# Second pair's k on ScalarE's queue, and the first weight piece rounded one slot later, in a fused attention and MLP kernel

## The chip, the cores and the metric

The kernel runs on one core of a Trainium2 chip. The metric is the device time of one execution in microseconds (us), the median of several runs. A profiled execution also gives its own span, from the first instruction to the last; times inside the kernel are counted from the start of that span.

## The reference

For each of 8 batches and 12 heads, with a sequence of 448 and a head dimension of 64, q and k are divided by their root mean square and scaled by gains, attention is computed with softmax, and the heads are put side by side. The result (3584 x 768) goes through two matrices with a pointwise function between them.

```python
q_n, k_n = (rmsnorm(q, g_q), rmsnorm(k, g_k))
scores = scale * np.matmul(q_n, k_n.transpose(0, 1, 3, 2))
attn = softmax(scores)
x = heads_side_by_side(np.matmul(attn, v))      # 3584 x 768
h = x @ w_in                                     # 768 x 2048, float64
return (h - np.tanh(h)) @ w_out                  # 2048 x 768, float64
```

The softmax and the joining of heads are abbreviated here. q, k and v are float32; the two weight matrices come as float64, and the kernel reads each number as two 32-bit words.

## The kernel before

The work on attention goes pair by pair: a pair is two heads of one batch, so there are 48 pairs, numbered 0 to 47 in this text. The kernel is one program written out by hand for each engine; the order in the source is the order on each engine's queue, and the framework adds the semaphore waits.

Six pairs make a batch. The MLP of a batch can only start when its six pairs are through, so the first batch is computed in "first slots" (`first_slot`, with s from -3 to 5), which have no MLP work beside them. A slot s holds the steps of several pairs: the scores and exps of pair s+1 (`scores`, exps at L504 on ScalarE), the transposes of k and q of pair s+2 (`turn`, L415 and L419 on TensorE, with the copies kT at L417 and qT at L423 on ScalarE), the squares of pair s+3 (`squares`, L123 and L124 on ScalarE, summed at L133 on VectorE, raised to the power -1/2 at L135 on GpSimd), the loads of q and k of pair s+4 and of v of pair s+2, and for pair s the sums over keys (`totals`, L572, with the reciprocal rs at L577), the weighted values (`last_values` L539, `values` L551) and the division (`divide`, L585).

After this, each first slot rounds some of the weights. A weight piece is 256 rows or columns of one half of a matrix: 128 partitions by 768 float64 numbers. There are 32 pieces. `weight_load` fetches the words of a piece; for the first eight pieces they land in the buffer named gT, which has room for four of them. `weight(to)` goes on until `to` pieces have been started: two ScalarE instructions for a piece (`round_weight_a`, L71 and L72), three VectorE instructions for the piece before it (`round_weight_b`, L78, L79, L82), one on GpSimd (`round_weight_c`, L90), and then the loads of up to four pieces ahead. With eight early pieces and six pairs, slot s asks for `weight(s + 3)`: none in slot -3, piece 0 in slot -2, piece 1 in slot -1, and so on. The first load of piece 0 is issued before the slots start.

All loads in question are issued by SyncE (SP). A load of q is one DMA of 224 KB. A load of k is four DMAs: two of 96 KB (L116) and two of 32 KB (L118). A load of v is one of 192 KB (L110) and two of 32 KB (L118). A weight piece of w_in is four DMAs of 192 KB (L265). The framework hands out eight DMA semaphores, in turn; an issue on a semaphore waits until the DMA that used it before has landed.

PSUM has eight banks. Three of them (named mm) are taken in turn by the transposes of k in `turn`, by the totals and by the two value sums; five (named sc) by the scores and by the transposes of q. `turn(s + 2)` in slot s takes the mm bank that the second half of the values of pair s takes again in the same slot, so those values wait for the copy kT.

Of the kernel before, what the change touches and what calls it, by code (L numbers as in the profile page):

```python
# [67 lines left out]
def round_weight_a(nc, raw, dst):  # L68

    lo, hi = raw[:, :, 0], raw[:, :, 1]  # L70
    nc.scalar.activation(dst, hi.bitcast(F32), AF.Abs, scale=2.0**-16)  # L71
    nc.scalar.mul(lo, lo.bitcast(U32), 2.0**-29)  # L72


def round_weight_b(nc, raw, dst):

    bits = dst.bitcast(I32)
    nc.vector.tensor_scalar(out=dst, in0=dst, scalar1=HI_MIN, scalar2=HI_MAX, op0=ALU.max, op1=ALU.min)  # L78
    nc.vector.tensor_scalar(  # L79
        out=bits, in0=bits, scalar1=4, scalar2=1, op0=ALU.logical_shift_left, op1=ALU.logical_shift_right  # L80
    )
    nc.vector.scalar_tensor_tensor(  # L82
        out=bits, in0=raw[:, :, 1], scalar=-(2**31), in1=bits, op0=ALU.bitwise_and, op1=ALU.bitwise_or
    )
# [5 lines left out]
    nc.gpsimd.tensor_tensor(out=bits, in0=bits, in1=raw[:, :, 0], op=ALU.add)  # L90


def fetch(nc, name, t, pair, in_order=False):

    S = pair.shape[1]
    P = 128
    KF, KR = S // P, S % P
    if name == "q":
        nc.sync.dma_start(
            out=t.rearrange("p h c d -> p h (c d)"), in_=pair.rearrange("h (p c) d -> p h (c d)", c=NCH)  # L100
        )
        return
    full, rest = pair[:, : KF * P].rearrange("h (p c) d -> h p c d", c=KF), pair[:, KF * P :]
    if name == "v":
        last = t[:, :, KF]
    if in_order:
        for h in range(2):
            nc.sync.dma_start(out=t[:, h, :KF], in_=pair[h, : KF * P].rearrange("(c p) d -> p c d", p=P))
    elif name == "v":
        nc.sync.dma_start(  # L110
            out=t[:, :, :KF].rearrange("p h c d -> p h (c d)"), in_=full.rearrange("h p c d -> p h (c d)")
        )
    else:
        last = t[:, KF]
        for h in range(2):
            nc.sync.dma_start(out=t[:, :KF, h], in_=full[h])  # L116
    for r in range(2):
        nc.sync.dma_start(out=last[r * KR : (r + 1) * KR], in_=rest.rearrange("h p d -> p h d"))  # L118


def squares_of(nc, sq, n, q, k):
# [16 lines left out]
def bounded_path(tc, ctx, q, k, v, moe_w_in, moe_w_out, out, g_col, ident, ones, half_ones, neg_half, early):  # L138
# [17 lines left out]
    nc = tc.nc  # L156
    B, H, S, D = q.shape
    DFF, DM = moe_w_out.shape
    P = 128
    CP = S // NCH  # L160
    NP = H // 2
    CD, CF = DM // P, DFF // P
    HALF = DM // 2
    FULL = S // P
    REST = S - FULL * P
    steps = [(b, hp) for b in range(B) for hp in range(NP)]
    NS = len(steps)
    EARLY, PIECES = 8, 2 * CF
    HS = S // 2
    HC, HF = CD // 2, CF // 2  # L170
# [4 lines left out]
    KF, KR = S // P, S % P  # L175
# [27 lines left out]
    def mm_bank():  # L203
        return bank_of("mm")
# [3 lines left out]
    def load(s, names):  # L208
        b, hp = steps[s]
        for name in names:  # L210
            src = {"q": q, "k": k, "v": v}[name]
            if s == 0 and name != "v":
                t = early[name]
            else:
                shape = [CP, 2, NCH, D] if name == "q" else [P, NCH, 2, D] if name == "k" else [P, 2, NCH, D]
                t = nat.tile(shape, F32, name=f"{name}_nat", bufs=3 if name == "v" else 2)
                fetch(nc, name, t, src[b, 2 * hp : 2 * hp + 2], by_blocks(s))
            loaded[name, s] = t


# [33 lines left out]
    def weight_load(n):  # L254

        f, i, _ = weight_piece(n)
        if n < EARLY:
            raw = stage[:, n % NSTAGE * 2 * DM : (n % NSTAGE + 1) * 2 * DM]
        else:
            raw = wp.tile([P, 2 * DM], I32, name="w_raw", bufs=3)  # L260
        if n < CF:
            rows = w_in_words[i * HALF : (i + 1) * HALF, f * 2 * P : (f + 2) * 2 * P]
            rows = rows.rearrange("(c h m r) f -> m h r c f", c=HC, h=2, m=2)
            for r in range(4):
                nc.sync.dma_start(  # L265
                    out=raw[r * BL : (r + 1) * BL].rearrange("p (c f) -> p c f", c=HC), in_=rows[r // 2, r % 2]
                )
        else:
            nc.sync.dma_start(
                out=raw.rearrange("p (f c) -> p f c", f=2),  # L270
                in_=w_out_words[f * P : (f + 2) * P, 2 * i * HALF : 2 * (i + 1) * HALF].rearrange(
                    "(f p) c -> p f c", p=P
                ),
            )
        raws[n] = raw.rearrange("p (n w) -> p n w", w=2)

    def weight_dst(n):
        return weight_piece(n)[2].rearrange("p f n -> p (f n)")
# [5 lines left out]
    def place_free(n):  # L284

        if n < EARLY:
            return n - NSTAGE < done[2]
        return n - 3 < max(done[2], EARLY)

    def weight(to):  # L290

        while done[1] < min(to, PIECES):
            n = done[1]
            round_weight_a(nc, raws[n], weight_dst(n))
            if n:
                round_weight_b(nc, raws[n - 1], weight_dst(n - 1))
            done[1] = n + 1
            finish_weights(n)
            while done[0] < min(n + 4, PIECES) and place_free(done[0]):
                weight_load(done[0])  # L300
                done[0] += 1
            if kept[1] < kept[0] and n >= 4 * kept[0] + 2:
                keep_weights()
        if done[1] == PIECES > done[2]:
            round_weight_b(nc, raws[PIECES - 1], weight_dst(PIECES - 1))
            finish_weights(PIECES)

    def finish_weights(to):
        while done[2] < to:
            round_weight_c(nc, raws.pop(done[2]), weight_dst(done[2]))  # L310
            done[2] += 1
            if done[2] % 4 == 0 and done[2] <= CF:
                combine_weights(done[2] // 4 - 1)
            keep_w_out(done[2] - 2)
# [14 lines left out]
    def keep_weights():  # L329
        j = kept[1]  # L330
        for p in ORDER:
            nc.sync.dma_start(out=w_in_dram[j, p].rearrange("p (f n) -> p f n", f=2), in_=built(j, p))
        kept[1] = j + 1
# [59 lines left out]
    def squares(s):  # L393
        squares_of(nc, early["sq"], early["n"], loaded["q", s], loaded["k", s])
# [35 lines left out]
    def by_blocks(s):  # L430
        return has(s) and steps[s][0] >= FIRST
# [51 lines left out]
    def sc_bank():  # L483
        return bank_of("sc")

    def scores(s, c):

        rr, kT, qT = turned[s]
        halves, keys, n = (1, P, S) if c < KF else (2, KR, HS)
        name, bufs = ("p", 2) if c < 2 else ("p_full", 1) if c < KF else ("p_last", 2)  # L490
        if c == 1:
            p = probs[s, 1] = probs[s, 0]
        else:
            p = probs[s, c] = pp.tile([P, 2, 2 if c < 2 else 1, n], F32, name=name, bufs=bufs)
        tiles = [sc_bank() for _ in range(2)]
        for i in range(halves):
            for h in range(2):
                r = slice(h * D, (h + 1) * D)
                nc.tensor.matmul(  # L499
                    tiles[h][i * keys : (i + 1) * keys, :n], lhsT=kT[r, c * P : c * P + keys],  # L500
                    rhs=qT[r, i * n : (i + 1) * n], start=True, stop=True,
                )
        for h in range(2):
            nc.scalar.activation(  # L504
                p[:, h, c if c < 2 else 0, :], tiles[h][:, :n], AF.Exp,
                scale=1.0 if rr is None else rr[:, 0, 2 * c + h : 2 * c + h + 1],
            )
# [339 lines left out]
    def has(s):  # L847
        return 0 <= s < NS

    def first_slot(s):  # L850

        if has(s + 1):
            scores(s + 1, 0)
            scores(s + 1, 1)
        if has(s + 2):
            turn(s + 2, mm_bank(), sc_bank())
        if s > -3:
            load(s + 4, "qk")
        if s > -3:
            squares(s + 3)  # L860
        norm(s + 3)
        if has(s):
            totals(s, mm_bank())
        if has(s + 2):
            load(s + 2, "v")
        if has(s + 1):
            scores(s + 1, KF)
        if has(s):
            av = [mm_bank() for _ in range(2)]
            last_values(s, av)  # L870
            values(s, av)
        if has(s + 1):
            scores(s + 1, 2)
            add(s + 1)
            add_last(s + 1)
        norm_q(s + 3)
        if s == -3:
            early["g_col"]()
        if has(s):
            divide(s, av)  # L880
        weight(EARLY * (s + 3) // (NP + 2))
        combine(2)

    def early_slot(s):
# [432 lines left out]
```

## Time and profile before

| what | value |
|---|---|
| time, 3 runs | 1428.47, 1431.7, 1432.04 us; median 1431.7 us |
| span of the profiled execution | 1429.6 us |
| TensorE matmul busy, 0 to 1429.6 us | 1396.1 us |
| TensorE idle, 0 to 20 us | 11.2 us of 20 |
| ScalarE idle, 0 to 30 us | 12.9 us of 30 |
| DMA traffic, whole span | 249.73 MB, 175 GB/s |

The idle times come from the busy times of ten-microsecond windows: TensorE was busy 2.07 and 6.71 us in the first two, and ScalarE 3.91, 5.53 and 7.71 us in the first three. A busy time is a sum over instructions; it says nothing on which of them the end of the program hangs. For that there is the chain of waits, which goes back from the last instruction to what released it, step by step. In the middle and at the end of the span that chain runs along TensorE; at the start it goes through other engines and transfers.

### The profile page before, as it was taken

The page shows a single profiled execution, that of the slowest core. Times are in us where ns is not written, and L with a number is a line of the kernel's source. Part 1 is how long each engine was busy: PE and PEld are TensorE (multiplying, and loading weights), DVE is VectorE, ACT ScalarE, POOL GpSimd, SP SyncE. Part 2 cuts the span into 40 slices and gives each one's busy share as a digit, 9 for nine tenths or more (in the row PEclk, how much of TensorE's full clock was granted, in tenths as well). Part 3 has the DMA queues.
Part 4 walks back from the last instruction along what each step waited for, and adds up shares of the span by engine and source line. Part 5 has one row for each costly group of instructions (what it writes and reads, how often), then busy time and mean ns, then how long its engine had stood idle before and what let it go on. Part 6 is the DMA issues. An engine that isn't in the chain of part 4 may idle for free.

```text
span 1429.6 us, 25681 instructions
## 1 busy us (share of the span) xinstructions
PE 1396.1 (98%) x10032; PEld 1174.7 (82%) x10032; DVE 867.8 (61%) x1396; ACT 412.0 (29%) x790; POOL 530.6 (37%) x348
## 2 busy tenths in 40 slices
PE   6999899999999999999999999999999999999997
PEld 3568654478998899889889988988998898899997
DVE  3999889856645676556755567546765577522311
ACT  5765454233311322222221223113221222201100
POOL 4656555232521345215533246313452145401310
PEclk9999899999999999999999999999999999999999
DMA  8769787864666656765657666666566656365663
GB/s 184 171 187 248 245 236 203 223 195 127 171 178 152 169 158 170 174 171 164 173 150 189 161 153 178 180 152 164 162 172 173 169 161 183 115 181 171 189 194 89
DMA packets 355254, 249.73 MB, mean 175 GB/s; under 512 B 266484, under 2 KB 297396, under 8 KB 355124
## 3 DMA queue, kind: packets, MB, share of 16 engines
q1 hardware_dynamic: 355120, 248.00, 64.0%
q8 instruction: 81, 1.33, 0.4%
q14 instruction: 49, 0.40, 0.1%
q10 hardware_dynamic: 4, 0.00, 0.0%
HBM read 214.50 MB, written 33.42 MB: 173 GB/s over the span
## 4 chain that ended last, share of the span: by engine, by line
PE 91%; DVE 3%; DMA 2%; SPq 1%; ACT 1%; issue 0%; POOL 0%; ACTq 0%
PE mm L640 66%; PE sc L499 9%; PE sc L551 6%; PE mm L805 4%; PE sc L572 2%; PE sc L539 2%; DMA k_nat<-in_k_dram 1%; DMA w_raw<-in_moe_w_out_dram 1%; DVE w_out L82 1%; DVE w_out L324 1%; DVE rs L577 1%; PE mm L551 1%; DMA gT<-in_moe_w_in_dram 0%; PE sc L419 0%; SPq L265 0%
## 5 line engine op out<-in xcount | busy, mean ns | idle before, releaser
L640 PE MATMUL mm<-xT,w_f 128*128 128x224 f32 x1392 | 275.6, 354 | 0.0
L640 PEld LDWEIGHTS mm<-xT,w_f 128*128 128x128 f32 x1392 | 262.1, 190 | 9.1 <-issue 7.8
L640 PE MATMUL mm<-gT,w_f 128*128 128x224 f32 x1344 | 263.0, 354 | 0.0
L640 PEld LDWEIGHTS mm<-gT,w_f 128*128 128x128 f32 x1344 | 252.8, 190 | 11.4 <-issue 9.1
L457 POOL TENSOR_TENSOR rr_mine<-rr_mine,neg_half 128x28 f32<-128x28 f32 x30 | 145.0, 4835 | 256.1 <-DVE rr_mine L456 256.1
L640 PE MATMUL mm<-tt,w_f 128*128 128x224 f32 x1044 | 208.7, 353 | 0.0
L640 PEld LDWEIGHTS mm<-tt,w_f 128*128 128x128 f32 x1044 | 197.0, 190 | 3.9 <-issue 3.9
L640 PE MATMUL mm<-tg,w_f 128*128 128x224 f32 x1008 | 197.7, 352 | 0.0
L677 POOL TENSOR_TENSOR gT<-s,th 128x448 f32<-128x448 f32 x96 | 122.6, 1284 | 200.6 <-ACT th L676 198.5
L640 PEld LDWEIGHTS mm<-tg,w_f 128*128 128x128 f32 x1008 | 190.6, 190 | 0.0
L499 PE MATMUL sc<-qT,kT 64*128 64x448 f32 (+1 forms) x960 | 168.1, 499 | 12.0 <-ACT p_last L504 8.1
L499 PEld LDWEIGHTS sc<-qT,kT 64*128 64x128 f32 (+1 forms) x960 | 71.2, 167 | 83.6 <-issue 50.0
L600 POOL TENSOR_TENSOR tt<-xT,tt 128x224 f32<-128x224 f32 x23 | 17.1, 744 | 232.2 <-DVE xT L585 232.1
L676 ACT ACTIVATE th<-s 128x448 f32<-128x448 f32 x96 | 55.6, 579 | 135.3 <-DVE s L706 55.6
L577 DVE RECIPROCAL rs<-sc 128x224 f32<-128x224 f32 x42 | 65.3, 1556 | 42.6 <-PE sc L572 42.5
L504 ACT ACTIVATE p<-sc 128x448 f32<-128x448 f32 x120 | 55.6, 550 | 109.1 <-PE sc L499 109.1
L135 POOL TENSOR_TENSOR rr<-rr,neg_half 112x8 f32<-112x8 f32 (+1 forms) x36 | 59.6, 1676 | 56.8 <-DVE rr L134 56.5
L551 PE MATMUL sc<-p,v_nat 128*32 128x224 f32 x1344 | 79.1, 353 | 0.0
L805 PE MATMUL mm<-gT,w_out 128*128 128x448 f32 x192 | 76.8, 557 | 0.0
L585 DVE TENSOR_TENSOR xT<-sc,rs 64x224 f32<-64x224 f32 x168 | 65.2, 388 | 9.7 <-PE sc L551 2.3
L464 DVE TENSOR_TENSOR qk_n<-qk_nat,rr_mine 128x896 f32<-128x896 f32 x30 | 46.4, 1546 | 39.3 <-POOL rr_mine L457 38.7
L805 PEld LDWEIGHTS mm<-gT,w_out 128*128 128x128 f32 x192 | 37.0, 196 | 37.6 <-issue 36.2
(136 smaller groups left out, 1630.9 us busy)
## 6 DMA issues: line engine op xcount, KB each, us to landing
w_f<-w_in SPq DMA_DIRECT2D x196, 384.0 KB, 3.2
w_f<-w_out SPq DMA_DIRECT2D x147, 512.0 KB, 4.0
w_raw<-in_moe_w_out_dram SPq DMA_DIRECT2D x16, 768.0 KB, 5.1
out_dram<-th SPq DMA_DIRECT2D x192, 56.0 KB, 1.9
w_in<-w_out SPq DMA_DIRECT2D x21, 384.0 KB, 6.5
qk_nat<-in_q_dram SPq DMA_DIRECT2D x120, 56.0 KB, 2.3
qk_nat<-in_k_dram SPq DMA_DIRECT2D x120, 56.0 KB, 2.3
gT<-in_moe_w_in_dram SPq DMA_DIRECT2D x32, 192.0 KB, 4.1
```

The costliest lines, as they stand in the source:

```text
L135: nc.gpsimd.tensor_tensor(out=r, in0=r, in1=neg_half[:rows], op=ALU.pow)
L457: nc.gpsimd.tensor_tensor(out=mine, in0=mine, in1=neg_half[:, :1].to_broadcast([P, 2 * NJ]), op=ALU.pow)
L464: nc.vector.tensor_tensor(out=n.rearrange("p i j d -> p (i j) d"), in0=loaded.pop(("qk", s)).rearrange("p i j d -> p (i j) d"), in1=rr[:, ...
L499: nc.tensor.matmul(tiles[h][i * keys : (i + 1) * keys, :n], lhsT=kT[r, c * P : c * P + keys], rhs=qT[r, i * n : (i + 1) * n], start=True, ...
L504: nc.scalar.activation(p[:, h, c if c < 2 else 0, :], tiles[h][:, :n], AF.Exp, scale=1.0 if rr is None else rr[:, 0, 2 * c + h : 2 * c + h ...
L551: nc.tensor.matmul(av[n][r : r + BL, :HS], lhsT=v_nat[:, h, c, m * BL : (m + 1) * BL], rhs=p[c][:, h, n * HS : (n + 1) * HS], start=False, ...
L577: nc.vector.reciprocal(rs, dn[:, :HS])
L585: nc.vector.tensor_tensor(out=x[m * D : (m + 1) * D, n * HS : (n + 1) * HS], in0=av[n][m * D : (m + 1) * D, :HS], in1=rs[n * D : (n + 1) * ...
L640: nc.tensor.matmul(bank[:, f * HS : (f + 1) * HS], lhsT=w[:, c * width + f, :], rhs=moving[p](c), start=(first and f == 0 and c == 0), sto ...
L676: nc.scalar.activation(th, h, AF.Tanh, bias=0.0, scale=1.0)
L677: eng.tensor_tensor(out=g[:, rows, cols], in0=h, in1=th, op=ALU.subtract)
L805: nc.tensor.matmul(bank[:, :S], lhsT=w_out_row(f, n // HC)[:, n % HC * P : (n % HC + 1) * P], rhs=g[:, f, :], start=(f == 0), stop=(f == C ...
```

## The change

Two edits are made. Both act in the first slots only.

The first edit gives `fetch` a queue. The k of pair 1 (s == 1) is now issued by ScalarE, and all other loads by SP as before. `load(1, "qk")` is called before slot -3, so the four DMA issues stand on ScalarE's queue right behind the branch that opens this path, ahead of the first kT.

The second edit leaves out `weight` in slot -3 and -2. Slot -3 had asked for no piece. The call in slot -2 had put the first piece's rounding (L71, L72) ahead of the exps of pair 0, and behind it the loads of pieces 1, 2 and 3. Now slot -1 asks for two pieces in one call: piece 0, then the loads of pieces 1, 2 and 3, then piece 1. Both stand behind the exps of pair 0. On SP's queue the twelve DMAs of pieces 1 to 3 now stand behind the loads of q and k of pair 3 and v of pair 1, where they had stood ahead of them. The order of instructions on TensorE, VectorE and GpSimd stays as it was.

```diff
-def fetch(nc, name, t, pair, in_order=False):
+def fetch(nc, name, t, pair, in_order=False, queue=None):
 
+    queue = queue or nc.sync
...
-            nc.sync.dma_start(out=t[:, :KF, h], in_=full[h])
+            queue.dma_start(out=t[:, :KF, h], in_=full[h])
     for r in range(2):
-        nc.sync.dma_start(out=last[r * KR : (r + 1) * KR], in_=rest.rearrange("h p d -> p h d"))
+        queue.dma_start(out=last[r * KR : (r + 1) * KR], in_=rest.rearrange("h p d -> p h d"))
...
-                fetch(nc, name, t, src[b, 2 * hp : 2 * hp + 2], by_blocks(s))
+                queue = nc.scalar if s == 1 and name == "k" else nc.sync
+                fetch(nc, name, t, src[b, 2 * hp : 2 * hp + 2], by_blocks(s), queue)
...
-        weight(EARLY * (s + 3) // (NP + 2))
+        if s > -2:
+            weight(EARLY * (s + 3) // (NP + 2))
         combine(2)
```

More of the change, by code (lines that the diff above doesn't have):

```diff
@@ L98, in fetch @@
     if name == "q":
-        nc.sync.dma_start(
+        queue.dma_start(
             out=t.rearrange("p h c d -> p h (c d)"), in_=pair.rearrange("h (p c) d -> p h (c d)", c=NCH)
@@ L107, in fetch @@
         for h in range(2):
-            nc.sync.dma_start(out=t[:, h, :KF], in_=pair[h, : KF * P].rearrange("(c p) d -> p c d", p=P))
+            queue.dma_start(out=t[:, h, :KF], in_=pair[h, : KF * P].rearrange("(c p) d -> p c d", p=P))
     elif name == "v":
-        nc.sync.dma_start(
+        queue.dma_start(
             out=t[:, :, :KF].rearrange("p h c d -> p h (c d)"), in_=full.rearrange("h p c d -> p h (c d)")
```

## The prediction

> **What bounds the kernel now.** I read the page first: over the span TensorE carries the end.
>
> ```profile
> PE 1396.1 (98%) x10032; PEld 1174.7 (82%) x10032; DVE 867.8 (61%) x1396; ACT 412.0 (29%) x790; POOL 530.6 (37%) x348
> PE 91%; DVE 3%; DMA 2%; SPq 1%; ACT 1%; issue 0%; POOL 0%; ACTq 0%
> ```
>
> With 98% busy, only the start can move: TensorE's work is not changed. So next the chain in order of time, for the first 75 us.
>
> ```profile
> 11.10 5.25 DMA q_nat<-in_q_dram
> ...
> 20.15 6.42 DMA gT<-in_moe_w_in_dram
> 26.59 5.37 DMA k_nat<-in_k_dram
> ...
> 32.13 0.64 ACT sq L124
> ...
> 35.20 0.66 PE mm L415 x4
> ```
>
> Up to 32 us the end hangs on SP's row of issues and their landings: a DMA of piece 3 issued at 20.15 had to land before the last DMA of k of pair 3 went out on its semaphore at 26.59; it landed at 31.96 and the squares (L124) began at 32.13. From 35.20 the chain goes along TensorE. ScalarE's waits between 9 and 48 us:
>
> ```profile
> ACT w_out L71 <- DMA gT<-in_moe_w_in_dram: 4.5, 1, 4.5
> ...
> ACT n L123 <- DMA q_nat<-in_q_dram: 2.3, 1, 2.3
> ACT p_full L504 <- PE sc L499: 1.9, 1, 1.9
> ACT sq L124 <- DMA k_nat<-in_k_dram: 1.5, 1, 1.5
> ```
>
> The 4.5 us stand ahead of piece 0's rounding, the 2.3 and 1.5 ahead of pair 3's squares. The timeline of ScalarE places them:
>
> ```profile
> 15.63 0.89 ACT L71 ACTIVATE w_out<-gT 128x768 f32<-128x768 f32 x1 [4.47 <-DMA gT<-in_moe_w_in_dram]
> 16.41 0.86 ACT L72 ACTIVATE gT<-gT 128x768 int32<-128x768 uint32 x1
> 17.18 2.20 ACT L504 ACTIVATE p<-sc,rr 128x448 f32<-128x448 f32 x4
> ...
> 22.91 0.96 ACT L71 ACTIVATE w_out<-gT 128x768 f32<-128x768 f32 x1
> ```
>
> Pair 0's exps start 6 us after ScalarE was free (11.16). Piece 1 (L71 at 22.91) meets no wait: its DMAs went out from 16.37 and the last landed at 22.07. Windows cut at the clock's steps show TensorE's clock:
>
> ```profile
> 13.64:17.05 3.41, 0.97 (x8) 0.63 (x6) 0.25 (x1) 1.42 (x2) 1.13 (x1) 1.00 0.98 224
> 17.05:20.46 3.41, 2.60 (x12) 1.27 (x13) 0.00 (x0) 3.41 (x8) 0.00 (x0) 0.50 0.91 219
> 20.46:23.88 3.42, 3.42 (x10) 2.01 (x8) 1.97 (x5) 3.42 (x8) 2.02 (x2) 0.50 1.06 225
> ```
>
> After a window with 0.97 us of matmul it ran at half for two windows (the clock is the number before the last two).
>
> **What the skill says.** The Trainium skill, DMA: Bandwidth & Descriptors, "Issuing engines are not separate DMA queues": loads from several engines share the same 16 DMA engines, and a second issuer saves only issue time. The trace has about 0.65 us of SP per k DMA. TensorE: Matmul & The Clock Gate, "Part 1": an idle window of about 3.4 us halves the clock and a busy one restores it. The trace agrees, with 3.41 us windows.
>
> **Edit 1, k of pair 1 on ScalarE.** It takes four issues off SP: 4 x 0.65 = 2.6 us, 6.42 to 9.04. ScalarE branches at 5.98 and is idle until its first kT at 8.78, so four issues (6.03 to about 8.65) hide in that idle time; cost 0 to 0.1 us for the kT and qT behind them and the scores that wait for those. Not all of the 2.6 is had: the fourth DMA of piece 0 shares a semaphore with the first k DMA, which lands 2.7 us after its issue (so took its like before), at about 8.9. Then q of pair 2 goes out at 9.4, not 11.10: 1.7 us gained on SP. k may land later, its bytes now mixed with piece 0's: -0.3 to +0.6 us against 10.43. That is hidden: norm and turn of pair 1 wait for q's power on GpSimd (1.65 us, to 13.2), not for k's.
>
> **Edit 2, ScalarE.** Exps of pair 0 start at 11.2. Scores come from TensorE until about 13.4, so they end at 13.7; kT, qT, squares and the last exps took 3.67 us (19.24 to 22.91) and fit in 14 to 18.0. Piece 0 (in by 13) takes 1.55 us, to 19.6. Here ScalarE is 3.3 us ahead of before (22.91).
>
> **Edit 2, SP.** Now piece 1 has q, k of pair 3 and v of pair 1 ahead. From 9.4: q 0.45, k 2.65, v 1.95; q 0.45, k 2.65, v 1.95 = 10.1, so piece 1 starts at 19.5 against 16.37. Before, the last of such a piece landed 5.7 us after the first issue (22.07 - 16.37), and the one from 41.43 in 5.55. So piece 1 is in at 25.1; bounds 24.1 (SP meets no waits and k does not hold piece 0) and 26.5 (6.7, as piece 4 took from 29.96). ScalarE idles 5.5 us, and behind piece 1 (1.57 us) exps of pair 1 begin at 26.6, 2.1 us later than 24.48. So the 4.5 us wait is moved, not removed. Queued behind it: exps of pair 1, then kT of pair 2; the values of pair 0 on TensorE wait for that kT, as they take its bank. Pieces 2 and 3 land 26 to 32, ahead of their rounding at 34 and 43: hidden. q and k of pair 3 now land by 20, so the 2.3 and 1.5 us waits go.
>
> **Sum on the path.** kT of pair 2 ends at 29.35 (27.2 before). Then TensorE has 0.3 of last values, 2.4 of values, and 12 score records: 2.82 as at 41.65. That is 5.5 us: turn of pair 3 at 34.9, against 35.20 (it waited there for rs L577, which is now done by 33.5, since squares of pair 3 are 1.2 us earlier). So 2.1 lost, 2.4 regained: -0.3 us at full clock.
>
> But TensorE is done with its totals at about 21.2 and idle to 27.2. Six us hold a window emptier than the one at 13.64, so the clock will be at half when work resumes, until a busy window has passed: between about 30.3 and 33.7, as the windows' phase is free. From 29.4 half of that is lost: 0.45 to 2.15 us, I take 1.3. Below, a gate that opens at once: 0. Above, two more windows. Before, its half clock at 17 to 24 cost nothing, as ScalarE and SP set the pace.
>
> So +1.0 us on 35.20. From there TensorE, ScalarE (the 1.9 us wait above) and from 53 VectorE (55.48 of 57 us busy to 110) take turns with nothing idle; no later order changes; the shift stays. 1429.6 + 1.0 = 1430.6 for the profiled span, which lies 2.1 below the median of the runs; on the median, 1432.7.
>
> **Rivals.** *Faster: the second weight does not hold.* If piece 1 were in by 19.6, exps of pair 1 would start there, and ScalarE would next wait for piece 2 (28.6): exps of pair 2 at 30.2 instead of 35.94, -5.7: 1426.0. Speaking for it: SP's issues pace the landings, and the DMA engines were full (0.9 to 1.1) from 10 to 30 us largely with pieces 1 to 3. Against: 10.1 us of issues at measured durations. A landing between gives less, one for one; over 0.3% (4.3 us) needs about 20.
>
> *Slower: the clock.* Same place, TensorE from 27.2: if the clock stays at half through the 5.5 us behind the kT and the totals next to them, these cost 5.5 more, with piece 1 at 25.5: about +5.7, 1437.4. It decides from the point where two windows in a row are broken by waits, as at 17.05 (2.60 busy of 3.41 did not restore it).
>
> *No effect: SP gains nothing*, as the semaphore of piece 0's last DMA holds it, and both waits cancel: 1431.7.
>
> **Chances.** About 0.3% is what a measurement of this kernel can tell from no change. Forecast 0.48 (1432.7; same 0.45, slower 0.03); second weight does not hold 0.22 (faster 0.20, same 0.02); clock 0.22 (slower 0.19, same 0.03); no effect 0.08 (same). Sum: faster 0.20, same 0.58, slower 0.22. The range goes from 1426.5 to 1437.5: it takes in most of both rivals, and leaves out about 0.1 on each side. The forecast's own range is 1430.4 (landing 24.1, clock 0: -1.3) to 1435.0 (landing 26.5, clock 2.15: +3.3).
>
> **What would show it.** Right: L71 of piece 0 at about 18 with no wait; L71 of piece 1 with about 5.5 us of wait for gT, to 25; L123 and L124 of pair 3 with no DMA wait; clock 0.5 somewhere in 27 to 34; L415 of pair 3 at 35 to 37. Wrong: L71 of piece 1 before 23, or L415 of pair 3 before 33 or after 39, or a difference that arises behind 60 us.

## The result, and the profile after

| | before | after |
|---|---|---|
| time, median of 6 runs | 1430.09 us | 1436.14 us |
| lowest and highest | 1426.42, 1432.04 us | 1433.64, 1439.26 us |
| span of the profiled execution | 1429.6 us | 1431.8 us |
| turn of pair 3 on TensorE starts | 35.20 us | 42.28 us |

The ratio after / before is 1.0046, 95% interval 1.0025 to 1.0066: after is slower. The ratio lies above the 0.3% that the prediction takes as the least change a measurement can tell; the lower end of the interval lies a little below it. The time lies in the range of the prediction, on its slow side; "same", the likeliest of the three outcomes, did not come about. The profiled execution of after was the quickest of its six (1433.64 us). Lines behind the edits are numbered one or two higher than before: L125 is the squares of k (L124 before), L417 the turn (L415), L501 and L506 scores and exps (L499, L504), L553 the values (L551).

TensorE's work on the page is what it was:

```profile
PE 1395.3 (97%) x10032; PEld 1172.4 (82%) x10032; DVE 866.5 (61%) x1396; ACT 412.4 (29%) x790; POOL 531.2 (37%) x348
PE 90%; DVE 3%; DMA 3%; ACT 2%; SPq 1%; issue 1%; POOL 0%; ACTq 0%
```

So nothing was added to the long part; the time is in the start. ScalarE's waits between 9 and 48 us (total, times, longest):

```profile
ACT w_out L71 <- DMA gT<-in_moe_w_in_dram: 7.8, 1, 7.8
...
ACT sq L125 <- DMA gT<-in_moe_w_in_dram: 2.8, 1, 2.8
```

The waits for q and k of pair 3 are gone, as forecast. In place of the 4.5 us for piece 0 there are 7.8 us for a weight piece, and 2.8 us at the squares (L125), which no step of the prediction had. The timeline of ScalarE places them:

```profile
13.35 0.63 ACT L125 ACTIVATE sq<-k_nat 128x512 f32<-128x512 f32 x1 [2.82 <-DMA gT<-in_moe_w_in_dram]
13.89 2.19 ACT L506 ACTIVATE p<-sc,rr 128x448 f32<-128x448 f32 x4
...
20.49 0.89 ACT L71 ACTIVATE w_out<-gT 128x768 f32<-128x768 f32 x1
...
29.96 0.89 ACT L71 ACTIVATE w_out<-gT 128x768 f32<-128x768 f32 x1 [7.79 <-DMA gT<-in_moe_w_in_dram]
...
31.51 2.19 ACT L506 ACTIVATE p<-sc,rr 128x448 f32<-128x448 f32 x4
33.58 0.66 ACT L419 ACTIVATE kT<-mm,g_col 128x448 f32<-128x448 f32 x1
```

Piece 0 (20.49) meets no wait; piece 1 (29.96) meets a long one, and the exps of pair 1 behind it begin at 31.51, where they began at 24.48 before. The 2.82 us at L125 are the squares of pair 1, whose k is now ScalarE's; the releaser named is a weight DMA, but the last k DMA landed at 13.24. What TensorE has of it, on its timeline:

```profile
32.19 1.54 PE L501 MATMUL sc<-qT,kT 64*64 64x224 f32 x8 [7.25 <-ACT p L506]
...
35.19 1.72 PE L553 MATMUL mm<-p,v_nat 128*32 128x224 f32 x16
...
42.28 0.66 PE L417 MATMUL mm<-ident,k_nat 128*128 128x128 f32 x4
```

It idles 7.25 us, and resumes at half clock: its values (L553) take from 35.19 to 39.61. The windows show the clock, the number before the last two:

```profile
28.94:32.35 3.41, 0.16 (x1) 0.16 (x2) 0.00 (x0) 2.39 (x4) 0.00 (x0) 0.50 1.08 224
32.35:35.76 3.41, 3.41 (x32) 1.21 (x36) 0.54 (x1) 3.41 (x8) 0.00 (x0) 0.50 1.08 223
35.76:39.18 3.42, 3.42 (x44) 1.77 (x36) 3.35 (x7) 0.62 (x2) 2.99 (x2) 0.50 1.10 230
39.18:42.59 3.41, 3.41 (x23) 1.67 (x16) 3.18 (x7) 1.94 (x4) 0.24 (x1) 1.00 0.55 134
```

Same instruction against same instruction, after is 3.2 us later at the reciprocal of pair 0, 6.5 at that of pair 1, 7.2 at that of pair 2, and still 7.2 at 160 us. Then the distance falls, to 4.5 at 230 us and 2.7 from 300 us to the end. There the profiled execution of before has stretches of half clock of 10.24 us from 167.23 and 3.4 us each from 197.95 and 245.74, and that of after one of 6.83 us from 175.71. No edit acts there; which windows fall is taken to be chance in the two executions. The difference of the medians of six runs, 6.05 us, is nearer to 7.2 than to 2.7. In most of the runs below, too, the trace at 60 us shows a larger distance from before than the times do (8.0 us against 4.7 with nine extra matmuls); why is open.

### The profile page after: what moved, and what is told of

It is laid out like the page before. It is cut to its first block, busy times and chain, and to the rows that moved or that the text cites. A ratio compares the mean times of both kernels' runs of the same rounds, so it can differ in the third digit from the quotient of the medians.

```text
span 1431.8 us, 25680 instructions
## 1 busy us (share of the span) xinstructions
PE 1395.3 (97%) x10032; PEld 1172.4 (82%) x10032; DVE 866.5 (61%) x1396; ACT 412.4 (29%) x790; POOL 531.2 (37%) x348
## 4 chain that ended last, share of the span: by engine, by line
PE 90%; DVE 3%; DMA 3%; ACT 2%; SPq 1%; issue 1%; POOL 0%; ACTq 0%
PE mm L642 66%; PE sc L501 9%; PE sc L553 6%; PE mm L807 4%; PE sc L574 2%; PE sc L541 2%; DMA gT<-in_moe_w_in_dram 1%; DVE rs L579 1%; DMA w_raw<-in_moe_w_out_dram 1%; DMA k_nat<-in_k_dram 0%; ACT p L506 0%; DVE w_out L82 0%; SPq L119 0%; PE sc L421 0%; POOL w_out L90 0%
## 5 line engine op out<-in xcount | busy, mean ns | idle before, releaser
L501 PE MATMUL sc<-qT,kT 64*128 64x448 f32 (+1 forms) x960 | 167.2, 501 | 15.0 <-ACT p L506 7.2
L501 PEld LDWEIGHTS sc<-qT,kT 64*128 64x128 f32 (+1 forms) x960 | 70.5, 168 | 86.1 <-issue 51.2
L506 ACT ACTIVATE p<-sc 128x448 f32<-128x448 f32 x120 | 55.6, 550 | 109.1 <-PE sc L501 109.1
L553 PE MATMUL sc<-p,v_nat 128*32 128x224 f32 x1344 | 79.1, 353 | 0.0
L523 DVE TENSOR_TENSOR rows<-p 128x896 f32<-128x896 f32 x38 | 44.8, 1178 | 35.9 <-ACT p L506 35.8
```

The source lines that it names most:

```text
L501: nc.tensor.matmul(tiles[h][i * keys : (i + 1) * keys, :n], lhsT=kT[r, c * P : c * P + keys], rhs=qT[r, i * n : (i + 1) * n], start=True, ...
L506: nc.scalar.activation(p[:, h, c if c < 2 else 0, :], tiles[h][:, :n], AF.Exp, scale=1.0 if rr is None else rr[:, 0, 2 * c + h : 2 * c + h ...
L553: nc.tensor.matmul(av[n][r : r + BL, :HS], lhsT=v_nat[:, h, c, m * BL : (m + 1) * BL], rhs=p[c][:, h, n * HS : (n + 1) * HS], start=False, ...
```

## The experiments

Three theories, called A, B and C in the expectations. A: the loads of piece 1, put behind q, k and v on SP by the second edit, come so late that ScalarE stalls and the clock halves behind the stall. B: k on ScalarE's queue (the first edit) is what costs. C: the order on ScalarE costs by itself, piece 0 behind the exps and two pieces in a row, wherever the loads are. How much of A is the stall, and how much the half clock behind it, was open.

**The first edit alone.** In the changed kernel the second edit is undone:

```diff
-        if s > -2:
-            weight(EARLY * (s + 3) // (NP + 2))
+        weight(EARLY * (s + 3) // (NP + 2))
```

> Only the first edit: k of pair 1 on ScalarE, the weights as before. Theory A (the loss is the place of piece 1's loads on SP, so it is the second edit's): the fourth DMA of piece 0 still waits for the first k DMA, to about 10.5 us; piece 0's rounding starts about 1.5 us earlier than before (14 instead of 15.6), pieces 1 to 3 and then q and k of pair 3 go out about 1 us later; turn of pair 3 at 35.5 to 36.5 instead of 35.2; the time is 0 to 1.5 us over before. Theory B (the loss is the semaphore and the slow landing of a k issued by ScalarE, so it is the first edit's): most of the 6 us is here, turn of pair 3 at 40 or later.

Measured: ratio 0.9998 (0.9986 to 1.0010), median 1429.41 against 1430.83 us of before: no change that can be told. ScalarE's waits:

```profile
ACT sq L125 <- DMA gT<-in_moe_w_in_dram: 3.1, 1, 3.1
ACT n L124 <- DMA q_nat<-in_q_dram: 3.1, 1, 3.1
```

The wait at the squares of pair 1 comes with this edit (3.1 us here); so does the late k. The wait itself does no harm here: piece 0, which is rounded next, came earlier (14.30, before 15.63), and so did the exps of pair 0 (15.88, before 17.18). But the semaphore of the late k holds SP's first load of k of pair 2 until 13.05, where it went out at 11.57 before. The loads behind it are later too, q of pair 3 is waited for longer (3.1 us against 2.3), and the turn of pair 3 is at 37.48, not at the 35.5 to 36.5 expected; a half clock from 35.07 has a part in this. The trace is 2.3 us behind before from 53 to 160 us. The times don't show these 2.3 us: their interval goes from -2.0 to +1.4 us.

**The second edit alone**, with all loads on SP:

```diff
-                queue = nc.scalar if s == 1 and name == "k" else nc.sync
+                queue = nc.sync
```

> Only the second edit: all loads on SP, the first rounding behind the exps of pair 0. Theory A: q, k of pair 3 and v of pair 1 take SP from 16.4 to 21.3 us, piece 1 goes out from there and lands at 27 to 28.5; its L71 waits 5 to 8 us; exps of pair 1 at 29 to 30 instead of 24.5; turn of pair 3 at 38 to 40; the time is 3 to 5 us over before. Theory B: within 1 us of before.

Measured: ratio 1.0031 (1.0017 to 1.0046), 1435.65 against 1430.83 us; at 60 us it is 6.4 us behind before. Its ScalarE, then its TensorE:

```profile
28.63 0.89 ACT L71 ACTIVATE w_out<-gT 128x768 f32<-128x768 f32 x1 [7.78 <-DMA gT<-in_moe_w_in_dram]
```

```profile
41.44 0.66 PE L417 MATMUL mm<-ident,k_nat 128*128 128x128 f32 x4
```

The same stall, 7.8 us, ends 1.3 us earlier, and the turn of pair 3 stands at 41.44, not 42.28 (38 to 40 was expected). So the second edit makes nearly the whole loss; on top of it the first adds 0.8 us in the traces, which the times can't separate.

**Both edits, with the loads of pieces 1 to 3 put back ahead of q and k of pair 3**, the roundings left where the change has them:

```diff
         if s > -2:
             weight(EARLY * (s + 3) // (NP + 2))
+        elif s == -2:
+            while done[0] < 4:
+                weight_load(done[0])
+                done[0] += 1
```

> Both edits, but the loads of pieces 1 to 3 are issued at the end of slot -2, where they were before; only the rounding of piece 0 stays in slot -1. Theory A: piece 1 lands at about 23.5 and its L71 waits 1 to 2 us; q and k of pair 3 are behind the pieces again and are waited for until 33; turn of pair 3 at 35.5 to 36.5; the time is 0 to 1.5 us over before. Theory C (what costs is the order on ScalarE, two pieces rounded in one go ahead of the exps of pair 1): about as slow as the changed kernel, 5 to 7 us over before.

Measured: ratio 0.9997 (0.9989 to 1.0005). Its ScalarE, then its TensorE:

```profile
23.23 0.90 ACT L71 ACTIVATE w_out<-gT 128x768 f32<-128x768 f32 x1 [1.21 <-DMA gT<-in_moe_w_in_dram]
```

```profile
35.92 0.66 PE L417 MATMUL mm<-ident,k_nat 128*128 128x128 f32 x4
```

The rounding of piece 1 is at 23.23 with 1.2 us of wait, and the turn of pair 3 at 35.92. ScalarE's order is the changed one, and the loss is gone from the times (the trace is 0.8 us behind before at 60 us): theory C falls. q of pair 3 is waited for again (4.1 us at L124; 2.3 before the change).

**Only piece 1 put ahead, all loads on SP**: the same lines with `done[0] < 2`, and `queue = nc.sync`.

> All loads on SP; rounding of piece 0 in slot -1; the loads of piece 1 alone at the end of slot -2, those of pieces 2 and 3 behind the loads of pair 3. Theory A: piece 1 lands at 22 and its L71 starts at about 22 behind a wait of 2 us; exps of pair 1 at 23.7, kT of pair 2 at 26.4, q and k of pair 3 in by 26 and never waited for; turn of pair 3 at 32 to 33.5; the time is 2 to 3 us under before. Theory C: as slow as the changed kernel. If the clock is what costs, TensorE's idle stretch before the kT (21 to 24.5) leaves it at half, and the gain is at most 1 us.

Measured: ratio 0.9997 (0.9984 to 1.0010). Its ScalarE, then its TensorE:

```profile
22.32 0.90 ACT L71 ACTIVATE w_out<-gT 128x768 f32<-128x768 f32 x1 [1.44 <-DMA gT<-in_moe_w_in_dram]
...
25.97 0.64 ACT L419 ACTIVATE kT<-mm,g_col 128x448 f32<-128x448 f32 x1
```

```profile
27.56 1.72 PE L553 MATMUL mm<-p,v_nat 128*32 128x224 f32 x16
...
34.56 0.66 PE L417 MATMUL mm<-ident,k_nat 128*128 128x128 f32 x4
```

Neither piece 1 nor pair 3 has a long wait for a DMA, and kT ends at 26.61, 7.6 us sooner than in after. All the same the turn of pair 3 is only 0.6 us sooner than before the change. From the end of kT to that turn it took 7.95 us: TensorE was at half clock from 24.53 to 31.36, and 1.72 us is what 16 values take there (0.96 us at full clock). The 2 to 3 us of gain that theory A expected did not come; the outcome is the one that the expectation gives for a half clock that takes the gain.

**Work to hold the clock**, in the changed kernel, ahead of the stall. The extra matmuls fill a bank of PSUM that is written over afterwards; they add work and change no result.

```diff
+        if s == 0:
+            spare = banks["mm"][(turns["mm"] + 1) % 3]
+            for _ in range(9):
+                nc.tensor.matmul(spare[:, :S], lhsT=ident, rhs=turned[1][1], start=True, stop=True)
```

> The changed kernel with nine extra matmuls (448 columns, into a bank that the value sums overwrite) on TensorE behind the totals of pair 0, so that it isn't idle from 25 to 32 us. If the half clock behind that stall is a cost of its own: the clock is full from 32 us on, the values of pair 0 take 2.4 us instead of 4.5, turn of pair 3 is at 39.5 to 40.5 instead of 42.3; the time is 2 to 3 us under the changed kernel, 3 to 5 us over before. If only the wait for piece 1 counts: turn of pair 3 stays at 42 and the time at 6 us over before.

Measured: ratio 1.0033 (1.0021 to 1.0044). The nine ended at 30.7 us, TensorE idled 1.87 us, and the clock still fell, from 33.65 to 40.48; the turn of pair 3 stood at 43.07. It decides nothing on the clock's price. So twelve of them:

> The changed kernel with twelve extra matmuls instead of nine, since nine ended at 30.7 and left TensorE idle for 1.9 us, and the clock still went to half. If the half clock is a cost of its own: full clock from 32 us on, values of pair 0 in 2.4 us, turn of pair 3 at 40 to 41 instead of 42.3 to 43, the place of the reciprocals behind it 2 to 3 us earlier than in the changed kernel, the time 2 to 3 us under it. If only the wait for piece 1 counts: no difference to the changed kernel.

Measured: ratio 1.0025 (1.0015 to 1.0036), 1433.82 us against 1430.38; full clock from 22.67 us, where the trace's record of the clock begins, to 172.9 us. Its ScalarE and its TensorE:

```profile
31.06 0.90 ACT L71 ACTIVATE w_out<-gT 128x768 f32<-128x768 f32 x1 [8.11 <-DMA gT<-in_moe_w_in_dram]
...
34.72 0.64 ACT L419 ACTIVATE kT<-mm,g_col 128x448 f32<-128x448 f32 x1
```

```profile
35.92 0.96 PE L553 MATMUL mm<-p,v_nat 128*32 128x224 f32 x16
...
41.07 0.66 PE L417 MATMUL mm<-ident,k_nat 128*128 128x128 f32 x4
```

Piece 1 is rounded 1.1 us later than in after, and yet the turn comes 1.2 us sooner. From the end of kT (35.36) it is 5.71 us away; in after it was 42.28 - 34.24 = 8.04. So the half clock costs 2.3 us there, and the late landing of piece 1 the rest: with the clock held, the kernel is still slower than before.

**Is it ScalarE's queue that makes k late, or the company of the weights?** The first edit alone, with the load of piece 0 moved behind q and k of pair 2:

```diff
+        if s == -2:
+            weight_load(0)
+            done[0] = 1
...
-    weight_load(0)
-    done[0] = 1
```

> Only the first edit, and the load of piece 0 moved behind the loads of q and k of pair 2 on SP, so that no weight bytes are fetched beside the k that ScalarE issues; piece 0 is then late and this time says nothing. If the k DMAs were late because they shared the DMA engines with piece 0: they land at 8.8, 9.5, 10 and 10.5 as when SP issues them. If loads from ScalarE are slow by themselves: 10.5 to 13 as in the changed kernel.

The four DMAs of k of pair 1, issue and last landing in us:

| kernel | issued | landed |
|---|---|---|
| before (SP) | 6.42, 7.05, 7.71, 8.38 | 9.13, 9.85, 10.04, 10.43 |
| after (ScalarE) | 6.04, 6.78, 7.44, 8.12 | 10.52, 12.70, 12.98, 13.24 |
| first edit alone | 6.13, 6.83, 7.48, 8.16 | 10.03, 13.04, 13.32, 13.63 |
| this one | 6.19, 6.88, 7.54, 8.23 | 9.32, 10.71, 11.07, 11.53 |

Without piece 0 beside it, k from ScalarE's queue lands 0.7 to 2.3 us sooner than with the first edit alone; the two kernels differ only in the place of piece 0. Of the lag behind before, 0.2 of 0.9 us remain on the first DMA and 1.1 of 3.2 us on the last, now beside SP's q and k of pair 2. So the larger part is the sharing with piece 0, not the queue. This rests on one execution of each.

**Two versions that might beat both.** Piece 1 early, all on SP, and three extra matmuls for the clock:

> The version with piece 1 alone loaded early (all loads on SP) and three such extra matmuls behind the totals of pair 0. If the clock took the gain of that version: full clock from 25 us on, kT of pair 2 at 26.5 as there, turn of pair 3 at 31.5 to 33 instead of 34.6, the time 2 to 3 us under before. If not: turn of pair 3 at 34.5 and the time as before.

Measured: ratio 1.0003 (0.9992 to 1.0015). The turn of pair 3 was at 32.28 us at full clock, 2.3 us sooner than with piece 1 early alone; but then q and k of pair 4 were waited for (1.62 and 0.97 us), as their loads stand behind those of the next pieces. Of the 2.3 us, 1.2 are left at the turn of pair 4 (42.87 against 44.03). The times show no gain. So the loads were spread as well: two pieces ahead, not four, for the first ones.

```diff
-            while done[0] < min(n + 4, PIECES) and place_free(done[0]):
+            while done[0] < min(n + (2 if n < 4 else 4), PIECES) and place_free(done[0]):
```

> Piece 1 alone loaded early, three extra matmuls, and in the first four pieces loads run two pieces ahead instead of four, so that q and k of pair 4 go out ahead of piece 3. If the waits for q and k of pair 4 (1.6 and 1.0 us) took back the gain of the version with three extra matmuls: they go, turn of pair 4 at 41 to 42 instead of 42.9, the third reciprocal at 48 to 49 instead of 49.9 (51.0 before), the time 2 to 3 us under before. If later pieces come too late with loads two ahead: new waits at L71, and the time at or above before.

Measured: ratio 0.9984 (0.9975 to 0.9993), 1429.22 against 1430.38 us: a small gain. The turn of pair 4 is at 41.97. Without the extra matmuls:

> The same without the extra matmuls. If the clock matters there: third reciprocal at 50 to 51, time within 1 us of before. If the loads alone matter: as the version with extra matmuls, 2 to 3 us under before.

Measured: ratio 0.9991 (0.9983 to 0.9999), 1429.39 us. Between 9 and 48 us its ScalarE waits 1.3 us for a weight piece (L71) and 1.2 us for q (L124). In its trace the half clock lasted from 19.82 to 23.23 only, and it stays 2.3 us ahead of before at 60 us. The third reciprocal, that of pair 2, is at 48.69 us, against 48.42 with the extra matmuls and 50.97 before. So in the traces the place of the loads makes the gain, and the extra matmuls add little. In the times the interval ends just below 1. What both share is the second edit's order on ScalarE, without the first edit and with the loads of weights between those of q, k and v.

## Why the prediction was right, and where it was not

The time fell inside the range, but the sum behind the forecast does not lead there: it gave the turn of pair 3 a delay of 1.0 us, to 36.2, and 7.1 were measured (42.28). By the prediction's own signs that is wrong, as the turn came after 39. The range held because it had been drawn to take in the slower rival. So the place and the kind of the loss were foreseen, and that the number fell inside is in part luck.

**Right: the stall moves from piece 0 to piece 1.** 4.5 us ahead of piece 0 became 7.8 ahead of piece 1; the 2.3 and 1.5 us of pair 3 went; TensorE came back at half clock; the turn of pair 3 was the place where it ended on the path; the shift of 7.2 us made by the pair after it stayed to 160 us. The experiment with the loads put back shows the cause: same order on ScalarE, no loss.

**The term that was mis-sized: piece 1 "in at 25.1", bounds 24.1 and 26.5.** It was in at 29.86. Exps of pair 1 began at 31.51, not 26.6, and kT of pair 2 ended at 34.24, not 29.35: 4.9 us. The landing itself was 4.8 us late, in two parts.

- SP began piece 1 at 22.53, not 19.5. The step that failed is "the first k DMA, which lands 2.7 us after its issue (so took its like before)": it took 4.48 us, so SP stood before piece 0's fourth DMA until 10.54 and before q of pair 2 until 10.89, not 9.4. Then the first k DMA of pair 2 needed the semaphore of ScalarE's second, 12.70: 1.4 us more, which the prediction did not have. The chain of waits in order of time has the landing of the first k DMA, the issue that it held, and the first issue of piece 1:

```profile
6.04 4.48 DMA k_nat<-in_k_dram
10.54 2.83 DMA gT<-in_moe_w_in_dram
...
22.53 0.59 SPq L267
```

  SP's own waits in the first 30 us have both stops, at piece 0 (L267) and at k of pair 2 (L117):

```profile
SPq L267 <- DMA k_nat<-in_k_dram: 2.4, 1, 2.4
SPq L117 <- DMA k_nat<-in_k_dram: 1.4, 1, 1.4
```

  The 1.7 us gain for SP thus became a loss: with all on SP, piece 1 began at 21.36. The Trainium skill, DMA: Bandwidth & Descriptors, "Issuing engines are not separate DMA queues", says that loads from several engines share the same engines. The trace agrees, and it is stronger than the prediction made of it: k, mixed with piece 0, was to land -0.3 to +0.6 us from 10.43, and landed 2.8 us behind it (13.24).
- From its first issue piece 1 took 7.3 us, not 5.6 (second edit alone: 7.2). The parts of its last DMA landed from 27.84 to 29.86, 2.0 us apart, where those of piece 1 before lie 0.6 apart. In after, a packet of 16,384 bytes of the instruction queue ran for 1.16 us from 25.12, and in before only at 29.66, behind the pieces. In the second edit alone it ran at 21.93, and an issue of SP took 1.42 us at 21.99 instead of 0.43. That this packet holds one of the sixteen parts back is argued from the times only; no run moved it alone.

**"That is hidden", said of a late k, was wrong.** The norm and turn of pair 1 were not what mattered: the squares of k stand on ScalarE ahead of the exps of pair 0. Those began at 13.89, not 11.2, and piece 0 at 20.49, not 18. It cost nothing in the end, as piece 1 was later still. The prediction looked at what is queued on ScalarE behind L71, but not at what is queued behind the squares.

**The clock: 1.3 us taken, 2.3 measured** (8.04 against 5.71 us from kT to the turn), above the upper bound of 2.15 for one busy window. The Trainium skill, TensorE: Matmul & The Clock Gate, "Part 1", has the clock back after at least one busy window, and the prediction counted on one. Here the window from 32.35 was busy for 3.41 us, and the next one was still at half. Had the clock come back at 35.76, the loss from 34.24 on would have been about 0.8 us, half of the 1.5 us between; this is an estimate from these windows. The second window made it 2.3. The 5.5 us for the same work at full clock were right (5.71). The rival "the clock" named this, and came closest in time (1437.4), but with piece 1 at 25.5 and 5.5 us for the clock. It is the other way round: 4.9 us of the shift beyond the forecast come from the landing, about 1.2 from the clock (8.04 against 5.5 + 1.3).

**Sum.** 1.0 forecast + 4.9 + 1.2 = 7.1 us, against 42.28 - 35.20 = 7.1 at the turn of pair 3.

**Slips of the prediction that don't change this.** The bound of 26.5 for the landing does not come out of its own numbers (19.5 + 6.7 is 26.2). The ends of the half clock, 30.3 and 33.7, lie 0.3 us ahead of 27.2 plus one and two windows of 3.41 us; put right, the upper bound of the loss is 2.3, about what was measured, but with two busy windows and not one. The reciprocal that the turn waited for, 1.2 us earlier, would be done by 34.0, not 33.5. And the chain of before does not stay on TensorE from 35.20: it goes through ScalarE from 42.76 and through VectorE from 52.98, as a later passage of the prediction has it.

**The rivals.** "The second weight does not hold" fell: piece 1 was not in by 19.6 but at 29.86. "No effect" fell too. The forecast's own upper end, 1435.0, was passed by 1.1 us.

## What to carry to other kernels

A step that moves carries its loads with it: before moving a rounding behind other work, see what its prefetch is then queued behind, and move the rounding without the loads if it can be done. A load on a second engine's queue does not only share the DMA engines; where issues of both engines take turns at the same semaphores, a slow one holds the other engine's next issues. When a change makes TensorE idle for longer (1.9 us were enough in one run here), give the half clock behind it a price of its own, and allow for more than one busy window. And check what stands behind every instruction that waits, the small ones too.

## What the runs showed of the hardware

- Half clock lasted longer than one busy window: three windows (28.94 to 39.18) in after, and four (25.27 to 38.93) in the second edit alone, where the windows are:

```profile
25.27:28.68 3.41, 0.00 (x0) 0.00 (x0) 0.00 (x0) 0.05 (x1) 0.00 (x0) 0.50 0.96 231
28.68:32.09 3.41, 1.23 (x8) 0.58 (x8) 0.00 (x0) 3.41 (x6) 0.00 (x0) 0.50 1.07 241
32.09:35.51 3.42, 3.42 (x39) 1.35 (x40) 1.56 (x5) 2.96 (x7) 0.65 (x1) 0.50 1.07 239
35.51:38.93 3.42, 3.42 (x38) 1.66 (x32) 3.05 (x6) 0.00 (x0) 2.58 (x2) 0.50 1.14 239
```

  A busy window (32.09) is followed by another at half; before the change one busy window from 20.46 was enough. Two more traces have a nearly full window at half and then another (3.37 us busy with piece 1 alone early, 3.34 with nine extra matmuls). Why it differs stays open: a matmul counts as busy in the profile while it may wait inside. In after the sixteen last values at 33.66 took 1.59 us, more than twice the 0.61 of before at full clock.
- An idle stretch of 1.87 us, after nine extra matmuls, was enough to lose the clock for 6.8 us; with twelve, and no such stretch, it held. The clock window with that stretch held 1.54 us of matmul; the one ahead of the half clock of the last version held 1.89. So a window need not be idle for the clock to be lost behind it. In after a window with 2.82 us (22.12 to 25.53) was followed by full clock.
- The DMAs of k of pair 1, 96 and 32 KB, took 4.5 to 5.9 us from ScalarE in after, beside weight loads that SP issued at the same time, and 2.0 to 2.8 us in before, from SP ahead of those loads.
